# Token tile 1 on the ScalarE queue, and a later fill of block 1's second and third w1 chunks

## The chip, the cores and the metric

The kernel runs on one core of one Trainium2 chip. The metric is device time in microseconds (us) of one execution. The profile shows a *span*, from the first to the last instruction of the program, which is shorter than the time by some 2 us. "Same" means within 2%.

Engines: PE is TensorE (PEld its weight loads), DVE is VectorE, ACT is ScalarE, POOL is GpSimd, SP is SyncE. A "q" after an engine's name (ACTq) means its instruction stream, where DMA transfers are issued.

## The reference, cut to what matters

```python
xn = layernorm(x)                        # x: (1, 2048, 512) bf16
q  = (xn @ wq) in 32 heads of 128
k, v = the last 512 cached keys and values, 8 heads, each used by 4 query heads
s  = softmax(q k^T / sqrt(128)) v, heads joined, @ wo
g  = silu( silu(xn @ w1) @ w2 )          # w1: 512 x 1792, w2: 1792 x 512
out = x + s * g
```

## The kernel before

The 2048 tokens are handled as 4 blocks of 512, a block as 4 tiles of 128. Block 0 opens with its own layernorm and the first MLP layer for its tokens (`h_pair`). After that each step of the loop is one attention head of one block, and single MLP matmuls ("fill") are slipped between the attention's matmuls so that PE does not run out of work. Two places are touched.

**Place A, the start.** Tile 0 goes out in halves on two queues, tile 1 on a third, tiles 2 and 3 on ScalarE's; the w1 pieces follow on SyncE's.

```python
    with tc.manual_schedule(engines={ENG.PE, ENG.Activation, ENG.DVE, ENG.SP, ENG.Pool}):
        ...
        nc.sync.dma_start(x_blk[0][0:HP4, 0, :], x0v[0:HP4, 0, :])
        nc.scalar.dma_start(x_blk[0][HP4:P, 0, :], x0v[HP4:P, 0, :])
        nc.gpsimd.dma_start(x_blk[0][:, 1, :], x0v[:, 1, :])              # tile 1
        make_identity(nc, ident)
        nc.gpsimd.memset(neg_half, -0.5)
        NE = NEARLY * P                                                   # 512
        nc.sync.dma_start(w1_sb[0][:, :, 0 : NE // 2], w1v[:, :, 0 : NE // 2])      # piece a
        nc.sync.dma_start(w1_sb[0][:, :, NE // 2 : NE], w1v[:, :, NE // 2 : NE])    # piece b
        nc.scalar.dma_start(x_blk[0][:, 2:4, :], x0v[:, 2:4, :])          # tiles 2 and 3
        nc.sync.dma_start(w1_sb[0][:, :, NE:], w1v[:, :, NE : FH * P])              # piece c
        nc.sync.dma_start(w1_sb[1][:, :, 0:NE], w1v[:, :, FH * P : FH * P + NE])    # second half, piece 1
        ...
        stats(0, 0)                    # VectorE: statistics of tile 0, then of tile 1, in order
        stats(0, 1)
        for j in range(2):
            rstd_first(j)              # ScalarE
            center(0, j)               # VectorE
        warm_up(10)                    # PE: dummy matmuls
        ...                            # PE: transposes of tiles 0 and 1
        for i in range(2 * FH):
            h_pair(i, i // FH)         # PE: 8 matmuls on tiles 0 and 1 (i < 7), then on 2 and 3
            if i == 3:
                t2 = turn(2)           # PE: transposes of tiles 2 and 3
                t3 = turn(3)
                ...
```

**Place B, the fill list.** `mlp_units` gives for a block a list `hs` of 14 x 4 matmuls (14 chunks of w1 columns, 4 matmuls each, one PSUM bank per chunk) and a list `os_` for the second layer. All use PSUM tag "f", which has two buffers. A chunk's bank is free again once ScalarE's tanh and one VectorE operation have read it. `pump(n)` issues the next n units.

```python
        fill = []
        for b in range(NBLK):
            hs, os_ = mlp_units(b, lambda i: "f")
            fill += hs * (b > 0) + os_
        ...
        def pump(n):
            nonlocal done
            for _ in range(n):
                if fill:
                    fill.pop(0)()
                    done += 1
```

The softmax here doesn't subtract the row's maximum and nothing guards it: scores larger than these inputs give would overflow.

Of the kernel before, what the change touches and what calls it, by code (L numbers as in the profile page):

```python
# [22 lines left out]
def kernel(  # L23
# [12 lines left out]
    nc = tc.nc  # L36
# [8 lines left out]
    ND = D // P  # L45
# [21 lines left out]
    warm = const.tile([P, BLK], BF16, name="warm")  # L67
    nc.vector.memset(warm, 0.0)
    ident = const.tile([P, P], BF16, name="ident")
    scratch = const.tile([P, 1], FP32, name="scratch")  # L70
    nc.vector.memset(scratch, 0.0)
    eps = const.tile([P, 1], FP32, name="eps")
    nc.vector.memset(eps, 1e-5)
    neg_half = const.tile([P, BLKT], FP32, name="neg_half")

    wq_sb = [res.tile([P, ND, REP * DH], BF16, name=f"wq{g}", tag=f"wq{g}") for g in range(HKV)]
    kT = [res.tile([P, W], BF16, name=f"kT{g}", tag=f"kT{g}") for g in range(HKV)]
# [13 lines left out]
    x_blk = {}  # L91
# [69 lines left out]
    def mlp_units(b, tag_of):  # L161

        cur = {}

        def h_unit(f, c):
            if (f, c) == (0, 0):
                new_hT(b)
            if c == 0:
                cur["ps"] = ps.tile([P, BLK], FP32, name="h_ps", tag=tag_of(f), bufs=PS_BUFS[tag_of(f)])
            h_mm(cur["ps"], b, f, c, 0, BLK)  # L170
            if c == ND - 1:
                h_evac(cur["ps"], b, f)

        def o_unit(j, f):
            if f == 0 and j == 0:
                g_sb[b] = res.tile([P, BLKT, D], BF16, name=f"gate{b}", tag=f"g{b}")
            if f == 0:
                cur["ps"] = ps.tile([P, D], FP32, name="oB_ps", tag=tag_of(j), bufs=PS_BUFS[tag_of(j)])
            nc.tensor.matmul(  # L179
                cur["ps"],  # L180
                hT[b][f // 2][:, f % 2, j * P : (j + 1) * P],
                w2_sb[f // FH][:, f % FH, :],
                start=(f == 0),
                stop=(f == NFC - 1),
            )
            if f == NFC - 1:
                th = work.tile([P, D], BF16, name="th", bufs=2)
                nc.scalar.activation(th, cur["ps"], ACT.Tanh, scale=0.25)
                nc.vector.scalar_tensor_tensor(  # L189
                    out=g_sb[b][:, j, :], in0=th, scalar=1.0, in1=cur["ps"], op0=ALU.add, op1=ALU.mult  # L190
                )

        hs = [lambda f=f, c=c: h_unit(f, c) for f in range(NFC) for c in range(ND)]
        os_ = [lambda j=j, f=f: o_unit(j, f) for j in range(BLKT) for f in range(NFC)]
        return hs, os_
# [417 lines left out]
    with tc.manual_schedule(engines={ENG.PE, ENG.Activation, ENG.DVE, ENG.SP, ENG.Pool}):  # L613
        new_x(0)
        x0v = x2[ds(0, BLK), :].rearrange("(j p) d -> p j d", p=P)
        nc.sync.dma_start(x_blk[0][0:HP4, 0, :], x0v[0:HP4, 0, :])  # L616
        nc.scalar.dma_start(x_blk[0][HP4:P, 0, :], x0v[HP4:P, 0, :])
        nc.gpsimd.dma_start(x_blk[0][:, 1, :], x0v[:, 1, :])
        make_identity(nc, ident)
        nc.gpsimd.memset(neg_half, -0.5)  # L620
        NE = NEARLY * P
        nc.sync.dma_start(w1_sb[0][:, :, 0 : NE // 2], w1v[:, :, 0 : NE // 2])  # L622
        nc.sync.dma_start(w1_sb[0][:, :, NE // 2 : NE], w1v[:, :, NE // 2 : NE])
# [95 lines left out]
        fill = []  # L719
        for b in range(NBLK):  # L720
            hs, os_ = mlp_units(b, lambda i: "f")
            fill += hs * (b > 0) + os_
        n_mlp = len(fill)
        done = 0

        def pump(n):
            nonlocal done
            for _ in range(n):
                if fill:
                    fill.pop(0)()  # L730
                    done += 1

        wo_plan = {
            HQ - 5: [(0, 4)],
# [35 lines left out]
        for s in range(NSTEP):  # L770
            b, h = divmod(s, HQ)
# [21 lines left out]
            if b == 0:  # L793
                units = S[0:1] + qu + S[1:2] + pu[:2] + S[2:3] + pu[2:] + S[3:4]
                for i, u in enumerate(units):
                    u()
                    pump((i + 1) * n // len(units) - i * n // len(units))
            else:
                for u in S[0:1] + qu + S[1:2] + pu + S[2:3]:
                    u()  # L800
                pump(2)
                S[3]()
                pump(2)
# [46 lines left out]
```

## Time and profile before

| | before |
|---|---|
| time, median of 3 runs | 550.3 us (549.86 to 550.56) |
| span of the profiled execution | 548.5 us |
| PE busy | 542.2 us, 99% of the span |
| granted clock of PE | 1.00 in the early stretches shown below |

The page of the kernel before, its first line, the first group of part 1 and part 4 (the chain of work that ended last, by engine):

```profile
span 548.5 us, 8534 instructions
PE 542.2 (99%) x2676; PEld 261.2 (48%) x2676; DVE 458.3 (84%) x1258; ACT 392.3 (72%) x1125; POOL 21.1 (4%) x42
...
PE 96%; DMA 1%; DVE 1%; SPq 0%; issue 0%; ACT 0%
```

PE is the limit. The view of the waits of PE from 0 to 46 us (us in total, times, longest):

```profile
PE warm_ps L642 <- DVE eps L73: 1.2, 1, 1.2
PE t_ps L649 <- DVE x_114 L122: 0.8, 1, 0.8
PE h_ps L691 <- DMA w_0_106<-in_B_w_dram: 0.2, 1, 0.2
PE h_ps L146 <- DVE gate_413 L189: 0.2, 1, 0.2
```

The second line is place A, the fourth is place B. The timeline of the start (columns: start, busy us, engine, line, operation, output<-input, and in brackets the idle time before with what ended it) shows why PE waits at A:

```profile
1.25 0.71 POOL L618 DMA_DIRECT2D x_114<-in_A_x_dram  x1 [0.81 <-POOLq L834]
...
4.85 0.69 DVE L107 BATCH_NORM_STATS2 st<-x_114 128x6 f32<-128x512 bf16 x1 [0.60 <-DMA x_114<-in_A_x_dram]
...
6.11 0.40 PE L649 MATMUL t_ps<-ident,x_114 128*128 128x128 bf16 x4 [0.83 <-DVE x_114 L122]
...
7.34 1.91 PE L691 MATMUL h_ps<-xnT_102,w_0_106 128*128 128x256 bf16 x16
...
9.44 1.49 PE L691 MATMUL h_ps<-xnT_102,w_0_106 128*128 128x256 bf16 x12 [0.20 <-DMA w_0_106<-in_B_w_dram]
...
11.39 0.61 PE L658 MATMUL t_ps<-ident,x_114 128*128 128x128 bf16 x8
```

Tile 1 is issued at 1.25 us and VectorE waits for it until 4.85 us; PE's first transposes come at 6.11 us after 0.83 us of idleness. Later, at 9.44 us, PE waits for a weight transfer all the same. The transposes of tiles 2 and 3 at 11.39 us will serve below as the mark of where the start ends.

DMA issues between 0 and 6 us (kind, count, KB, us from issue to landing), and the line of GB/s of that window in 40 slices of 0.15 us:

```profile
x_114<-in_A_x_dram POOLq DMA_DIRECT2D x1, 128.0 KB, 3.6
x_114<-in_A_x_dram ACTq DMA_DIRECT2D x1, 256.0 KB, 3.7
w_0_106<-in_B_w_dram SPq DMA_DIRECT2D x1, 384.0 KB, 6.6
...
GB/s 0 0 0 0 0 0 0 0 0 0 0 0 0 41 191 185 212 198 130 178 184 314 246 307 321 403 301 273 328 317 290 345 352 335 324 328 294 266 220 183
```

Place B, the timeline of VectorE and PE around 42 us:

```profile
41.58 0.68 DVE L189 SCALAR_TENSOR_TENSOR gate_413<-th,oB_ps 128x512 bf16<-128x512 bf16 x1
...
41.75 0.38 PE L146 MATMUL h_ps<-xnT_103,w_0_106 128*128 128x512 bf16 x1
42.30 0.38 PE L146 MATMUL h_ps<-xnT_103,w_0_106 128*128 128x512 bf16 x1 [0.18 <-DVE gate_413 L189]
```

Pipelined matmuls of this shape start 0.216 us apart in this stretch. Here the starts are 0.55 us apart, so the wait for the bank that `gate_413` empties costs 0.34 us, more than the recorded 0.18 us of idleness.

### The profile page before, as it was taken

What the parts mean: (1) busy time and instruction counts of PE and PEld (TensorE: products, weight loads), DVE (VectorE), ACT (ScalarE), POOL (GpSimd) and SP (SyncE); (2) the same over time, 40 slices, a digit from 0 to 9 for tenths busy, and PEclk for the clock granted to TensorE, in tenths of its full rate; (3) what the DMA queues carried; (4) which work ended last, traced back from release to release, by engine and by line L of the source; (5) the groups of instructions that cost most, each with busy time, mean ns of one, the idle gap of its engine ahead of it and who ended that gap; (6) DMA issues with size and microseconds to landing.
All of it is one profiled execution on the core that took longest, in us unless ns stands there. A gap on an engine that the chain in (4) does not pass through costs nothing.

```text
span 548.5 us, 8534 instructions
## 1 busy us (share of the span) xinstructions
PE 542.2 (99%) x2676; PEld 261.2 (48%) x2676; DVE 458.3 (84%) x1258; ACT 392.3 (72%) x1125; POOL 21.1 (4%) x42
## 2 busy tenths in 40 slices
PE   8999999999999999999999999999999999999997
PEld 5644444444444444444444444444444444444586
DVE  6878888887886688898889888988889889988897
ACT  5558767766785677777777777777788888888600
POOL 1000010000000000010001000100010000100010
PEclk9999999999999999999999999999999999999999
DMA  8969669797849799989887988898888878888921
GB/s 270 261 115 190 151 136 163 147 164 149 167 89 185 178 213 220 199 161 190 162 149 149 183 167 141 162 184 160 148 162 179 153 153 157 186 154 154 173 78 39
DMA packets 298813, 89.69 MB, mean 164 GB/s; under 512 B 282352, under 2 KB 297840, under 8 KB 298768
## 3 DMA queue, kind: packets, MB, share of 16 engines
q1 hardware_dynamic: 297056, 85.02, 79.4%
q0 software_dynamic: 1360, 3.80, 2.7%
q8 instruction: 21, 0.34, 0.2%
q10 hardware_dynamic: 352, 0.33, 0.2%
q14 instruction: 24, 0.20, 0.1%
HBM read 17.30 MB, written 2.10 MB: 35 GB/s over the span
## 4 chain that ended last, share of the span: by engine, by line
PE 96%; DMA 1%; DVE 1%; SPq 0%; issue 0%; ACT 0%
PE o_ps L275 20%; PE q_ps L210 20%; PE sc_ps L232 20%; PE s_ps L333 15%; PE oB_ps L179 8%; PE h_ps L146 7%; PE m_ps L476 4%; PE h_ps L691 2%; DMA w_0_106<-in_B_w_dram 1%; DVE gate_413 L189 0%; DVE p_all L247 0%; DVE st L107 0%; SPq L622 0%; DVE qT L222 0%; SPq L616 0%
## 5 line engine op out<-in xcount | busy, mean ns | idle before, releaser
L235 ACT ACTIVATE p_all<-sc_ps 128x512 bf16<-128x512 f32 x512 | 305.3, 597 | 104.3 <-PE sc_ps L232 100.3
L247 DVE TENSOR_SCALAR p_all<-p_all,rden 128x512 bf16<-128x512 bf16 x512 | 157.9, 351 | 9.1
L281 DVE CAST oT<-o_ps 128x512 bf16<-128x512 f32 x128 | 88.2, 689 | 35.8 <-PE o_ps L275 35.2
L235 ACT ACTIVATION_READ_ACCUMULATOR p_all<-sc_ps 128x1 f32 x512 | 100.4, 196 | 0.0
L232 PEld LDWEIGHTS <-qT 128*128 128x128 bf16 x512 | 50.1, 98 | 60.7 <-issue 0.5
L222 DVE CAST qT<-q_ps 128x512 bf16<-128x512 f32 x111 | 76.3, 687 | 3.3 <-PE q_ps L210 3.3
L333 PEld LDWEIGHTS <-oT 128*128 128x128 bf16 x384 | 37.6, 98 | 45.3
L245 DVE RECIPROCAL rden<-den 128x2 f32<-128x2 f32 x256 | 40.6, 158 | 11.2 <-ACT p_all L235 11.0
L156 ACT ACTIVATE th<-h_ps 128x512 bf16<-128x512 f32 x42 | 25.0, 595 | 4.0 <-PE h_ps L146 3.9
L333 PE MATMUL s_ps<-wo_big_2083,oT 128*128 128x512 bf16 x84 | 26.0, 379 | 0.0
L333 PE MATMUL s_ps<-wo_big_2084,oT 128*128 128x512 bf16 x84 | 26.0, 379 | 0.0
L333 PE MATMUL s_ps<-wo_big_2344,oT 128*128 128x512 bf16 x84 | 26.0, 379 | 0.0
L333 PE MATMUL s_ps<-wo_big_2345,oT 128*128 128x512 bf16 x84 | 26.0, 379 | 0.0
L232 PE MATMUL sc_ps<-kT_86,qT 128*128 128x512 bf16 x64 | 24.3, 379 | 0.0
L232 PE MATMUL sc_ps<-kT_87,qT 128*128 128x512 bf16 x64 | 24.3, 379 | 0.0
L232 PE MATMUL sc_ps<-kT_88,qT 128*128 128x512 bf16 x64 | 24.3, 379 | 0.0
L232 PE MATMUL sc_ps<-kT_89,qT 128*128 128x512 bf16 x64 | 24.3, 379 | 0.0
L232 PE MATMUL sc_ps<-kT_90,qT 128*128 128x512 bf16 x64 | 24.3, 379 | 0.0
L232 PE MATMUL sc_ps<-kT_91,qT 128*128 128x512 bf16 x64 | 24.3, 379 | 0.0
L232 PE MATMUL sc_ps<-kT_92,qT 128*128 128x512 bf16 x64 | 24.3, 379 | 0.0
L232 PE MATMUL sc_ps<-kT_93,qT 128*128 128x512 bf16 x64 | 23.9, 379 | 0.0
L350 POOL DMA_DIRECT2D out_dram<-x_e x12 | 6.6, 550 | 314.5 <-DVE rden L245 257.9
(317 smaller groups left out, 871.1 us busy)
## 6 DMA issues: line engine op xcount, KB each, us to landing
pT<-p_all SPq DMA_TRANSPOSE x128, 4.4
x_e<-in_A_x_dram POOLq DMA_DIRECT2D x12, 128.0 KB, 3.3
out_dram<-x_e POOLq DMA_DIRECT2D x12, 128.0 KB, 2.2
w_0_108<-in_B_w_dram SPq DMA_DIRECT2D x1, 896.0 KB, 9.5
w_1_109<-in_B_w_dram SPq DMA_DIRECT2D x1, 896.0 KB, 9.8
w_0_106<-in_B_w_dram SPq DMA_DIRECT2D x2, 256.0 KB, 4.8
w_1_107<-in_B_w_dram SPq DMA_DIRECT2D x1, 512.0 KB, 7.6
x_130<-in_A_x_dram SPq DMA_DIRECT2D x1, 512.0 KB, 9.6
```

The costliest lines, as they stand in the source:

```text
L146: nc.tensor.matmul(h_ps[:, lo : lo + n], w1_sb[f // FH][:, c, (f % FH) * P : (f % FH + 1) * P], xnT[b][:, c, lo : lo + n], start=(c == 0), ...
L156: nc.scalar.activation(th, h_ps, ACT.Tanh, scale=0.5)
L179: nc.tensor.matmul(cur["ps"], hT[b][f // 2][:, f % 2, j * P : (j + 1) * P], w2_sb[f // FH][:, f % FH, :], start=(f == 0), stop=(f == NFC - 1),
L210: nc.tensor.matmul(cur["ps"], wq_sb[h // REP][:, c, (h % REP) * DH : (h % REP + 1) * DH], xnT[b][:, c, :], start=(c == 0), stop=(c == ND - 1),
L222: nc.vector.tensor_copy(qT[s], cur["ps"])
L232: nc.tensor.matmul(sc, qT[s][:, j * P : (j + 1) * P], kT[h // REP], start=True, stop=True)
L235: nc.scalar.activation(p_all[s][:, :, j, :], sc.rearrange("p (kc q) -> p kc q", q=P), ACT.Exp, scale=INV_SQRT_DH, accum_out=den[s][:, j : ...
L245: nc.vector.reciprocal(rden, den[s][:, j0 : j1 + 1])
L247: nc.vector.tensor_scalar_mul(p_all[s][:, :, j, :], p_all[s][:, :, j, :], rden[:, j - j0 : j - j0 + 1])
L275: nc.tensor.matmul(cur["ps"], v_sb[h // REP][:, kc, :], pT[s][:, kc, :], start=(kc == 0), stop=(kc == NKC - 1))
L281: nc.vector.tensor_copy(oT[s // 2][:, s % 2, :], cur["ps"])
L333: nc.tensor.matmul(acc[j], oT[(b * HQ + h) // 2][:, h % 2, j * P : (j + 1) * P], wo_of(h), start=(h == 0), stop=(h == HQ - 1),)
```

## The change

Three parts. Tile 1 goes to ScalarE's queue, to be there earlier. The two constants are made on GpSimd before the hand-ordered part, since nothing precedes them there any more. In block 1, two empty turns are put before the second chunk, so that its bank is free when PE comes to it; the third chunk then catches up, two matmuls a turn.

```diff
     ident = const.tile([P, P], BF16, name="ident")
+    make_identity(nc, ident)
     ...
     neg_half = const.tile([P, BLKT], FP32, name="neg_half")
+    nc.gpsimd.memset(neg_half, -0.5)
...
-        nc.gpsimd.dma_start(x_blk[0][:, 1, :], x0v[:, 1, :])
-        make_identity(nc, ident)
-        nc.gpsimd.memset(neg_half, -0.5)
+        nc.scalar.dma_start(x_blk[0][:, 1, :], x0v[:, 1, :])
...
             hs, os_ = mlp_units(b, lambda i: "f")
-            fill += hs * (b > 0) + os_
+            if b == 1:
+
+                late = [lambda u=hs[i : i + 2]: [x() for x in u] for i in (2 * ND, 2 * ND + 2)]
+                fill += hs[:ND] + [None, None] + hs[ND : 2 * ND] + late + hs[3 * ND :] + os_
+            else:
+                fill += hs * (b > 0) + os_
...
                 if fill:
-                    fill.pop(0)()
+                    u = fill.pop(0)
                     done += 1
+                    if u is not None:
+                        u()
```

## The prediction

> **What bounds the kernel.** TensorE. The page gives PE 542.2 us of a 548.5 us span (99%), and the chain of waits that ended last is 96% PE. PE lacks work only before its first matmul (1.18 us), at a few points up to 11 us, once at 42 us, and in the closing evacuation. The change removes no matmul, so it can only win idle PE time, at two places.
>
> **Place A, the start (timeline 0 to 12 us).** Token tile 1 of x goes out on the GpSimd queue at 1.25 us and lands 3.6 us later; VectorE, in order, waits 0.60 us for it, until 4.85 us, and so centres tile 0 only at 5.67 us, although its rstd is ready at 4.57 us. PE idles 0.83 us before the first transposes (6.11 us); the first MLP matmul is at 7.34 us. On the ScalarE queue I expect the issue at about 1.3 us and landing near 4.3 us (the 64 KB piece there took 2.2 us, the 256 KB one 3.7 us). Tiles 2 and 3 go out 0.6 us later (one issue) and land near 5.5 us; their statistics start after 6.5 us, so that is harmless. First transposes and first MLP matmul come about 0.5 us earlier.
> But most of that is off the critical path: the chain runs through the third piece of w1's first half, issued at 2.78 us, landing at 9.44 us, where PE waits 0.20 us; next, the first piece of the second half holds a weight load at 10.94 us. From 3 us on the DMA engines are full (share about 1.0, 260 to 365 GB/s) and the bytes ahead of these pieces stay the same. The Trainium skill, "DMA: Bandwidth & Descriptors", section "Issuing engines are not separate DMA queues", says that all queues run on the same 16 engines, so another queue adds no bandwidth. PE will mostly wait longer near 9.4 us. Only what the weights land earlier counts: 0.2 us (0 to 0.5).
>
> **Place B, block 1's first MLP fill (40 to 46 us).** The only PE wait found after 11 us is at 42.30 us: the second w1 chunk needs the PSUM bank that VectorE empties (gate evacuation, 41.58 to 42.27 us). Recorded idle is 0.18 us; by start-to-start spacing (0.55 us against the usual 0.216) it is 0.34 us. In the changed order only one score matmul more stands between the first and second chunk, so the second is reached near 42.18 us: about 0.1 us of wait is left. The third, two at a time, catches up; from the fourth the order is as before. The fourth needs the second's bank: 0.57 us until tanh, 0.6 tanh, 0.69 VectorE puts that near 45.7 us, against a demand near 45.5 us, so up to 0.2 us can come back there. Net 0.15 us (0 to 0.3).
>
> **Moved for nothing:** identity and the -0.5 constant on GpSimd; done by 2.6 us, first needed at 6.1 and 9.3 us.
>
> **Sum.** 0.35 us off 550.3; the runs before spread by twice that. Predicted 549.9 us, range 549.2 to 550.6; chances: faster by over 2% 0.005, within 2% 0.99, slower 0.005.
>
> **What would show it.** Right: tile 1 lands before 4.5 us; first MLP matmul near 6.8 us; a longer PE wait for w1 near 9 us; the 42.3 us gap at about 0.1 us, perhaps a small new one near 45.6 us; all after 50 us shifted by a constant 0.2 to 0.6 us. Wrong: w1 landing half a microsecond earlier (the software queue was costing bandwidth: 549.4 or less) or later (tile 1 competes earlier), or a new gap near 45.6 us eating B.

## More of the kernel before

The output matrix `wo` is loaded in portions of rows by SyncE, each portion one transfer; two experiments join or split portions of this plan only to change the *number* of transfers.

```python
        wo_plan = {
            HQ - 5: [(0, 4)],
            HQ - 4: [(4, 3)],
            HQ - 3: [(7, 4)],
            HQ - 2: [(11, 3)],
            ...
```

## The result, and the profile after

| | before, same rounds | after |
|---|---|---|
| median of 6 runs | 549.99 us (549.33 to 550.56) | 549.95 us (549.88 to 550.32) |
| ratio | | 1.0001, 95% interval 0.9988 to 1.0014: same |
| profiled span | 548.5 us | 547.7 us |

A ratio is the mean time of one kernel's fast runs over that of the other's in the same rounds, so it is not quite the ratio of the medians in the table. The interval is about 0.7 us to either side.

The predicted number, 549.9 us, was met. Yet there is something to explain: the span fell by 0.8 us and the time by nothing. The page of the kernel after:

```profile
span 547.7 us, 8533 instructions
PE 542.2 (99%) x2676; PEld 261.1 (48%) x2676; DVE 458.4 (84%) x1258; ACT 392.1 (72%) x1125; POOL 20.5 (4%) x41
...
PE 98%; DMA 1%; SPq 0%; DVE 0%; issue 0%
```

The waits of PE from 0 to 46 us are down to two:

```profile
PE warm_ps L642 <- DVE eps L74: 1.2, 1, 1.2
PE h_ps L691 <- DMA w_0_111<-in_B_w_dram: 0.2, 1, 0.2
```

The timeline of the start, the same instructions as before:

```profile
1.32 0.60 ACTq L620 DMA_DIRECT2D x_119<-in_A_x_dram  x1
...
4.12 0.66 DVE L109 BATCH_NORM_STATS2 st<-x_119 128x6 f32<-128x512 bf16 x1
...
5.36 0.40 PE L649 MATMUL t_ps<-ident,x_119 128*128 128x128 bf16 x4
...
6.58 1.99 PE L691 MATMUL h_ps<-xnT_107,w_0_111 128*128 128x256 bf16 x16
...
8.72 1.48 PE L691 MATMUL h_ps<-xnT_107,w_0_111 128*128 128x256 bf16 x12 [0.16 <-DMA w_0_111<-in_B_w_dram]
...
10.68 0.61 PE L658 MATMUL t_ps<-ident,x_119 128*128 128x128 bf16 x8
```

Every mark is 0.7 us earlier, the first transposes (5.36 instead of 6.11 us) as well as the end of the start (10.68 instead of 11.39 us). Taken alone this reads as a full win of 0.7 us. The DMA issues of 0 to 6 us, and the GB/s of that window, say something else:

```profile
x_119<-in_A_x_dram ACTq DMA_DIRECT2D x1, 128.0 KB, 2.5
x_119<-in_A_x_dram ACTq DMA_DIRECT2D x1, 256.0 KB, 4.6
w_0_111<-in_B_w_dram SPq DMA_DIRECT2D x1, 384.0 KB, 5.9
...
GB/s 0 0 0 0 0 0 0 0 0 0 0 0 0 20 171 246 191 226 191 300 318 171 79 65 75 106 160 123 133 229 314 277 341 348 372 376 355 352 362 345
```

Tile 1 is at hand 2.5 us after its issue instead of 3.6. Tiles 2 and 3 take 4.6 us instead of 3.7. Between 3.3 and 4.2 us, where the kernel before moved some 300 GB/s, the DMA engines now move 65 to 160.

Place B after the change, PE's timeline:

```profile
41.03 0.38 PE L148 MATMUL h_ps<-xnT_108,w_0_111 128*128 128x512 bf16 x1
41.25 0.38 PE L234 MATMUL sc_ps<-kT_91,qT 128*128 128x512 bf16 x1
41.59 0.38 PE L148 MATMUL h_ps<-xnT_108,w_0_111 128*128 128x512 bf16 x1
...
44.61 0.38 PE L277 MATMUL o_ps<-pT,v_99 128*128 128x512 bf16 x1
44.89 0.38 PE L148 MATMUL h_ps<-xnT_108,w_0_111 128*128 128x512 bf16 x1
```

By spacing, the wait ahead of the second chunk is now 0.34 - 0.216 = 0.12 us (it was 0.34), and a new one of 0.28 - 0.216 = 0.06 us stands ahead of the fourth chunk.

So there were three questions. Is the 0.7 us of the start real? What is B worth over the whole kernel? And where does the time go between the span and the time?

### The profile page after: what moved, and what is told of

Read it like the earlier page. It is cut to its first block, busy times and chain, and to the rows that moved or that the text cites. A ratio compares the mean times of both kernels' runs of the same rounds, so it can differ in the third digit from the quotient of the medians.

```text
span 547.7 us, 8533 instructions
## 1 busy us (share of the span) xinstructions
PE 542.2 (99%) x2676; PEld 261.1 (48%) x2676; DVE 458.4 (84%) x1258; ACT 392.1 (72%) x1125; POOL 20.5 (4%) x41
## 3 DMA queue, kind: packets, MB, share of 16 engines
q0 software_dynamic: 1312, 3.67, 2.6%
## 4 chain that ended last, share of the span: by engine, by line
PE 98%; DMA 1%; SPq 0%; DVE 0%; issue 0%
PE o_ps L277 20%; PE q_ps L212 20%; PE sc_ps L234 20%; PE s_ps L335 15%; PE oB_ps L181 9%; PE h_ps L148 7%; PE m_ps L478 4%; PE h_ps L691 2%; DMA w_0_111<-in_B_w_dram 1%; SPq L622 0%; SPq L618 0%; SPq L623 0%; PE t_ps L658 0%; DVE m_4_6595 L502 0%; DVE x_t L604 0%
## 5 line engine op out<-in xcount | busy, mean ns | idle before, releaser
L277 PE MATMUL o_ps<-pT,v_100 128*128 128x512 bf16 x64 | 18.4, 379 | 0.0
```

The costliest lines, as they stand in the source:

```text
L277: nc.tensor.matmul(cur["ps"], v_sb[h // REP][:, kc, :], pT[s][:, kc, :], start=(kc == 0), stop=(kc == NKC - 1))
```

## The experiments

All kernels gave the right result. The letters in the expectations are these theories. **Q**: tile 1's earlier landing gains the whole 0.7 us seen in the first two profiles. **J**: the first profile of the kernel before fell on an execution with a late start, and the real gain is smaller. For what lies outside the span: **G**, it hangs on GpSimd's instruction stream; **S**, on ScalarE's; **C**, on the constants made early. **R**: the end of the program waits through a fixed list, and one more transfer moves the last output in it. **W**: the w1 pieces land later because the early transfers use two queues instead of three.

### Both kernels again, and each half of the change alone (5 rounds each)

e1 is the kernel before and e2 the kernel after, both unchanged. e3 is the change without its fill part; e4 is the kernel before with only the fill part.

```diff
# e3, against the kernel after
-            if b == 1:
-                ...
-                fill += hs[:ND] + [None, None] + hs[ND : 2 * ND] + late + hs[3 * ND :] + os_
-            else:
-                fill += hs * (b > 0) + os_
+            fill += hs * (b > 0) + os_
# e4, against the kernel before: the same lines the other way round, queue and constants as before
```

> The kernel before, unchanged, as a second look at its start. Theory J (jitter): the landing of the third w1 piece (9.44 us in the first profile) moves by half a microsecond or more from execution to execution, whatever the kernel, and the span with it; then this profile shows another landing time, and span minus landing time is the same as in the first profile (548.5 - 9.44 = 539.1 us) within 0.1 us. Rival Q (the queue really gains 0.7 us, the equal medians are chance): landing again at 9.4 us, span 548.5 us, and the kernel after is 0.8 us faster in this job.

> The changed kernel again. Theory Q: third w1 piece lands near 8.7 us again, span 547.7 us, 0.8 us under the kernel before. Theory J: the landing differs from 8.72 us; span minus landing stays at 547.7 - 8.72 = 539.0 us; mean time within 0.3 us of the kernel before.

> Only the queue of token tile 1 (and the earlier GpSimd constants); the fill order as before. The wait at 42 us (0.34 us by spacing) is back whole. Theory Q: span about 547.8 to 547.9 us, 0.6 to 0.7 us under before. Theory J: mean time equal to before within 0.3 us; first transposes near 5.4 us, but the third w1 piece wherever the DMA puts it. Prediction on record: 0.2 us faster.

> Only the fill order; token tile 1 stays on the GpSimd queue. Both theories: the wait at 42 us shrinks from 0.34 to 0.12 us by spacing and 0.06 us comes back at the fourth chunk, so 0.16 us less from 40 to 46 us. Theory Q: time 0.16 us under before. Theory J: the same on average, but hidden in a spread of 0.5 us or more from the start.

| run | median us (range) | ratio to the kernel before, 95% interval |
|---|---|---|
| e1, before again | 549.69 (549.19 to 550.31) | 0.9985, 0.9968 to 1.0002 |
| e2, after again | 550.01 (549.72 to 550.21) | 0.9990, 0.9972 to 1.0008 |
| e3, queue only | 550.41 (549.67 to 551.1) | 0.9997, 0.9980 to 1.0015 |
| e4, fill only | 549.8 (549.34 to 550.0) | 0.9985, 0.9969 to 1.0002 |
| the kernel before beside them (11 runs) | 550.33 (549.33 to 552.75) | |

The kernel before against itself gave 0.9985, so that is the size of the noise: none of these times tells the parts apart. The traces do. This is the page's first line and PE's timeline of the start in the repeated run of the kernel before (e1):

```profile
span 547.7 us, 8534 instructions
...
5.64 0.40 PE L649 MATMUL t_ps<-ident,x 128*128 128x128 bf16 x4 [0.20 <-DVE x L122]
6.87 3.88 PE L691 MATMUL h_ps<-xnT,w 128*128 128x256 bf16 x32
10.58 0.61 PE L658 MATMUL t_ps<-ident,x 128*128 128x128 bf16 x8
```

The same kernel that had started its first transposes at 6.11 us and ended its start at 11.39 us now does so at 5.64 and 10.58 us, and its span is 547.7 us, that of the changed kernel. In this execution no wait of PE for w1 is recorded: its 32 matmuls run on from 6.87 us, in 3.88 us (3.65 us in e6, e8, e9 and e11). The six spans of e1 lie between 547.4 and 548.5 us; those of e2 between 547.4 and 547.9. In e2 the third w1 piece landed at 8.83 us, close to the 8.68 us of the first look, as Q had expected too; it is e1 that decides. J stands and Q falls: the first profile of the kernel before was a late one.

From block 1's first fill matmul to VectorE's last operation, on the other hand, the trace gives the same number every time for each fill order:

```
fill order   kernel    first fill matmul   last VectorE op   difference, us
old          before         40.67              545.24            504.57
old          e1             39.86              544.42            504.56
old          e3             40.05              544.62            504.57
new          after          39.95              544.36            504.41
new          e2             40.12              544.52            504.40
new          e4             40.09              544.49            504.40
```

B is worth 0.16 us, which is what the two gaps at 42 and 45 us add up to (0.34 - 0.12 - 0.06). From PE's transposes of tiles 2 and 3 to that first fill matmul it is 29.28 us in before (11.39 to 40.67) and in e1 (10.58 to 39.86), and 29.27 us in after. So the trace is rigid from 11 us to VectorE's last operation, and the start can be read from one mark.

In e4, which has the old start, time minus span was small again; in e3, which has the new start, it was as in e2. That led to the next set.

### What lies outside the span (e5 in 5 rounds, e6 to e8 one look each)

Time minus span is 2.29 us (2.23 to 2.40, 24 runs) in the kernels in which tile 1 left GpSimd's queue with nothing in its place (after, e2, e3, e6, e10), and 1.78 us (1.72 to 1.89, 59 runs) where GpSimd issues an early load. These four runs were to say which engine's stream it hangs on. All edits are small:

```diff
# e5: the kernel after, with two dummy memsets, so that GpSimd's stream is as long as before
+    pad = const.tile([P, 1], FP32, name="pad")
+    for _ in range(2):
+        nc.gpsimd.memset(pad, 0.0)
# e6: the kernel before, tile 1 on SyncE's queue
-        nc.gpsimd.dma_start(x_blk[0][:, 1, :], x0v[:, 1, :])
+        nc.sync.dma_start(x_blk[0][:, 1, :], x0v[:, 1, :])
# e7: the kernel before, with make_identity and the memset of neg_half moved up as in the change
# e8: the kernel before, with one more instruction on ScalarE
         nc.scalar.activation(scratch, scratch, ACT.Tanh)
+        nc.scalar.activation(scratch, scratch, ACT.Tanh)
```

> The changed kernel with two dummy GpSimd memsets at its start, so that GpSimd has 70 instructions again as before the change (68 in the changed kernel). In all runs so far the time lies 1.79 us over the span of the program's own instructions with token tile 1 on the GpSimd queue, and 2.30 us with it on the ScalarE queue: half a microsecond is given back outside the span. Theory G (it hangs on the length of GpSimd's instruction stream): 1.8 us again, and the time 0.5 us under the changed kernel, near 549.5 us. Theory S (on ScalarE's stream, one instruction longer) and theory C (on the early constants): 2.3 us, time near 550.0 us.

> The kernel before with token tile 1 on the SyncE queue: GpSimd two instructions shorter, ScalarE as before, constants where they were. Time minus span: theory G 2.3 us; theories S and C 1.8 us.

> The kernel before with only the identity and the -0.5 constant made early; token tile 1 still on the GpSimd queue, behind them. Time minus span: theory C 2.3 us; theories G and S 1.8 us. At the start token tile 1 lands later than in the kernel before (about 0.3 us), and by theory J the third w1 piece and the first transposes of tiles 2 and 3 still fall into the range seen so far (10.6 to 11.4 us for the latter).

> The kernel before with one more ScalarE instruction (the table-warming tanh on 128x1 twice, 0.2 us). Time minus span: theory S 2.3 us; theories G and C 1.8 us.

| run | instructions on GpSimd | time us | span us | time minus span us |
|---|---|---|---|---|
| before | 70 | 550.36 (profiled run) | 548.5 | 1.78 (mean of 59 runs of its kind) |
| after | 68 | 549.95 (profiled run) | 547.7 | 2.29 (mean of 24 runs of its kind) |
| e5 | 70 | 549.95 median, 549.71 to 550.21 | 548.3 | 1.77 (6 runs, 1.72 to 1.81) |
| e6 | 68 | 550.34, one run | 548.0 | 2.34 |
| e7 | 70 | 549.97, one run | 548.2 | 1.77 |
| e8 | 70 | 549.44, one run | 547.7 | 1.74 |

(The count is of all records of GpSimd's stream, issues and register work included, and so is above the 42 and 41 of the page.) G stands: two idle memsets bring the difference back to 1.77 us, and neither ScalarE's stream (e8) nor early constants (e7) change it; e6, with ScalarE's stream untouched, has the large difference. S and C fall. One expectation of e7 was missed: tile 1 landed at 4.68 us there, not later than in before (4.82 us); its mark, 11.07 us, lay in the range expected.

But I had expected e5 to take 549.5 us, and it took 549.95, as the kernel after does. Half a microsecond came back outside the span and the span grew. The semaphore records of SyncE at the end of the program say how. Times are ns before the end of the span; each line of waits is worked through by SyncE in the order given:

```
before  last output issued -2817
        waits: -2421 S105, -2367 S106 S104, -2306 S107 S103, -2242 S109 S102, -2180 S111 S101,
               -2121 S112 S100, -2059 S114 S99, -2000 S115 S108, -1938 S117 S113, -1260 S118 S116
        the last output's landing counts S118 up until -1277; SyncE drains -1192, -1132
after   last output issued -2867
        waits: -2470 S117, -2417 S118 S116, -1310 S100 S115, -1246 S102 S114, -1184, -1125,
               -1063, -1004, -943, -883 S110 S109
        the last output's landing counts S100 up until -1327; SyncE drains -816, -756
```

SyncE waits for all semaphores in a fixed order, some 62 ns each. The hardware queues' transfers take eight of these semaphores in turn. Before, the last output of the kernel had the eighth, S118, and all other waits were done while it was still on its way: 0.145 us after it had landed (-1277 to -1132) SyncE was through. Tile 1 on ScalarE's queue is one more transfer of this kind, so every later one moves by one, the last output comes to the first of the eight, S100, and seven more waits have to be worked through *after* it has landed: 0.571 us (-1327 to -756). The view of SyncE's waits from 543 us on shows the same, before and after:

```profile
SPq L845 <- DMA out_dram<-x_t: 0.6, 1, 0.6
...
SPq L852 <- DMA out_dram<-x_t: 1.1, 1, 1.1
```

Before, SyncE comes to the wait for the last output when the others are done, and waits 0.6 us; after, it comes to it earlier, waits 1.1 us and still has seven waits to go. This is theory R. It costs 0.571 - 0.145 = 0.43 us. e5 has the same 0.571 us (-1713 to -1142); it hid in the span there.

And G is mostly a move. With 70 instructions GpSimd waits 0.41 us inside the span ahead of the last barrier, with 68 it waits 0.04 us there and a gap after the span is 0.5 us longer. From SyncE's second drain to the end of the time it is 1.13 + 1.79 = 2.92 us before and 0.76 + 2.29 = 3.05 us after: 0.13 us to the bad. In the single profiled runs this stretch takes 2.89 to 2.99 us with 70 instructions (9 runs, e5 among them) and 3.03 to 3.12 us with 68 (5 runs). What is waited for after the span, the trace doesn't show.

### Changing the number of transfers (e10 in 5 rounds, e11 one look), and two more

R can be tried without touching the start at all. e10 joins two loads of `wo` in the kernel after, so that the last output is back on the eighth semaphore. e11 adds four transfers to the kernel before, so that it comes to the fourth.

```diff
# e10, against the kernel after
-            HQ - 3: [(7, 4)],
-            HQ - 2: [(11, 3)],
+            HQ - 3: [(7, 7)],
# e11, against the kernel before
-            HQ - 5: [(0, 4)],
-            HQ - 4: [(4, 3)],
+            HQ - 5: [(0, 1), (1, 1), (2, 1), (3, 1)],
+            HQ - 4: [(4, 1), (5, 2)],
```

> The changed kernel with two loads of wo in the middle (4 and 3 heads) made one of 7 heads: one hardware-queue transfer fewer, as many as before the change; its start is untouched and GpSimd keeps 68 instructions. Theory R: last landing to drain 0.14 us, time minus span still 2.3 us, time 0.43 us under the changed kernel, near 549.6 us. Theory Q2 (the end is longer because of what the start does): 0.57 us, time 550.0 us.

> The kernel before with two loads of wo in the middle cut into six: four hardware-queue transfers more. Theory R: the last output takes the fourth of the eight semaphores, four more waits of 62 ns follow its landing, so landing to drain is 0.14 + 0.25 = 0.39 us; time minus span 1.8 us. Q2: 0.14 us.

| run | last output landed, to SyncE's second drain | expected by R |
|---|---|---|
| e10 | 0.144 us (-906 to -762) | 0.14 |
| e11 | 0.386 us (-1533 to -1147), fourth of the eight, S112 | 0.39 |
| e8, for comparison (same number of transfers as before) | 0.144 us | 0.14 |
| e6, for comparison (same number as after) | 0.570 us (-1332 to -762) | 0.57 |

SyncE's wait in e10 is the short one again:

```profile
SPq L851 <- DMA out_dram<-x_t: 0.6, 1, 0.6
```

R is shown: one transfer fewer, at about 175 us, takes 0.43 us out of the end of the kernel. The time agrees: e10's median is 549.54 us (549.4 to 549.8, 5 runs), its mean 549.61 us, where the 12 runs of the kernel after have a mean of 550.03 us (standard deviation 0.18), 0.42 us more. Those were taken in other jobs (e2's on another chip), and against the kernel before of its own rounds e10 is 0.9992 (0.9979 to 1.0005), where e2 was 0.9990: set against their own rounds, the times do not tell the two apart. So the proof is the trace. e11 took 550.37 us in its one run, with a span of 548.5 us.

e9 tests the transfers at the start: tile 1 on ScalarE's queue as in the change, and tiles 2 and 3 on GpSimd's, so that three queues are used again. e12 is e4 once more.

```diff
# e9, against the kernel after
         nc.scalar.dma_start(x_blk[0][:, 1, :], x0v[:, 1, :])
+        nc.gpsimd.dma_start(x_blk[0][:, 2:4, :], x0v[:, 2:4, :])
...
-        nc.scalar.dma_start(x_blk[0][:, 2:4, :], x0v[:, 2:4, :])
```

> The changed kernel, but tiles 2 and 3 of block 0 go on the GpSimd queue while tile 1 stays on ScalarE's: as many hardware-queue transfers as before the change. Theory R (the end list): SyncE waits at the end for every semaphore in a fixed order; hardware-queue transfers take eight semaphores in turn, so one transfer more moves the last output from the last place of the list to the third, and seven more waits of 62 ns (0.43 us) run after it has landed. Here it is back at the last place: last landing to the SyncE drain 0.14 us as in the kernel before (0.57 in the changed one), GpSimd 70 instructions, time minus span 1.8 us. Start, theory W (the weights pay for tile 1: with two queues instead of three 400 to 450 KB are in at 4.5 us instead of 510 to 620): here three queues again, tile 1 lands before 4 us, the first w1 pieces by 6.1 and 7.2 us. Time near 549.5 us, 0.5 us under the changed kernel. Rival: no recovery at the end (end 0.57 us), time 550.0 us.

> The fill order alone again, to compare with the two repairs in one job. 0.16 us under the kernel before where their starts are alike; mean 549.7 to 550.1 us, with a wider spread (0.4 us or more) than kernels that load tile 1 on the ScalarE queue (0.18 us in twelve runs of the changed one).

e12 gave 550.03 us (549.52 to 550.19, 5 runs), ratio 0.9997 (0.9985 to 1.0009), and once more 545.02 - 40.62 = 504.40 us from the first fill matmul to the last VectorE operation. So the 0.16 us of B is exact in every trace and invisible in the time.

e9 ran four times in 548.94 to 549.38 us, three of these the fastest runs of the whole study, and twice in 552.45 and 552.67 us, with a granted clock of 0.997 in both. Its ratio is 1.0004 (0.9981 to 1.0028). Its start ended at 10.33 us and its last output was on S118 again. Whether its typical gain would hold could not be settled: runs of over 551.2 us also came up in the kernel before (one at 552.75 us). There were 7 in 59 runs of kernels with an early load on GpSimd's queue, and none in 30 runs without one, though the slowest of these, one of e3 at 551.1 us, is just under that limit. That may be chance, and no run here was made to decide it.

### The start, over all traces

PE's start on the transposes of tiles 2 and 3, the mark of the start's end, and KB moved by the DMA engines up to 4.5 us:

```
tile 1 on GpSimd's queue     mark us   KB        tile 1 on ScalarE's queue   mark us   KB
before                        11.39    596       after                        10.68    402
e1                            10.58    602       e2                           10.84    454
e4                            10.81    612       e3                           10.77    454
e8                            10.55    514       e5                           10.92    438
e11                           11.13    559       e10                          10.92    415
e12                           11.34    564
mean                          10.97              mean                         10.83
range                          0.84              range                         0.24
(e7, constants early: 11.07, 618)                (e6, SyncE's queue: 10.82, 602; e9: 10.33, 532)
```

The new order gains 0.14 us in the mean, with a standard error of 0.16 us by the scatter of these marks: an estimate that is not clear of zero. What shows better is steadiness: the marks lie within 0.24 us instead of 0.84. In the times even that is not shown: e3, with the new start, ran from 549.67 to 551.1 us.

Why only so little, when tile 1 lands a whole microsecond earlier? The w1 pieces land later. Pieces a and b of its first half came at 5.65 to 6.37 and 6.61 to 7.21 us in the traces of the left column, and at 6.18 to 6.84 and 7.47 to 7.72 us in those of the right one. In the typical trace of either kernel it is then piece c that PE runs into: in 11 of the 14 traces the mark comes 2.00 to 2.03 us after c has landed (in e8, e9 and e11 later, 2.08 to 2.43 us). From its landing to the end of the span it is 539.12 us in before (548.51 - 9.39), 539.13 in e1, 539.00 in after (547.68 - 8.68), 539.02 in e2 and 538.96 in e4: with B's 0.16 us taken off, one constant. e8, where piece c landed at 8.12 us, is above it, 539.56 us, as PE itself was the limit there.

In after the later landing goes with the hole in the GB/s line between 3.3 and 4.2 us. In the trace, tiles 2 and 3 (issued at 1.95 us) get their first data only at about 4.2 us, and piece a, in packets of 512 bytes, has the engines nearly to itself: the first 288 of its packets start over 1.42 us, where in before they did so over 0.74. Theory W, that this comes of having two queues for three, stays open. e6 also used two and moved 602 KB by 4.5 us, as much as before, so two queues alone do not empty the engines; but there piece a was issued one transfer later (2.24 instead of 1.37 us), and pieces a, b and c landed as late as in the new order (6.82, 7.66 and 8.81 us). e9, with three queues, met W's expectation for pieces a and b (6.12 and 6.93 us), and not that for tile 1 (4.32 us instead of before 4). What the five traces of the new order share is an order: piece a, issued at 1.37 us, starts at 3.04 to 3.09 us, and tiles 2 and 3, issued at 1.95 us, only at 3.67 to 4.30 us; in before, tiles 2 and 3 were issued first and started at 2.59 us, piece a at 3.94 us. Whether the order or the number of queues counts, no run settled. The Trainium skill, "Perfetto Trace Analysis", section "DMA Instruction — HWDGE (DVE, Sync)", describes a block that makes descriptors, is shared by two sequencers (the page's diagram names VectorE's and SyncE's, its note SyncE's and ScalarE's, which issue here) and is locked by one of them while in use. The late first data of tiles 2 and 3 agree with that, but do not show it.

## Why the prediction was right or wrong

**The number: right by luck.** Predicted 549.9 us, measured 549.95 us. The prediction took 0.35 us off a base of 550.3 us, the median of three runs. With three runs more the base is 549.99 us, and of the predicted gain only 0.04 us shows in the medians (549.99 to 549.95 us in the same rounds), with an interval of 0.7 us to either side.

| term | predicted | measured | read from |
|---|---|---|---|
| A, the start | -0.2 us (0 to -0.5) | -0.14 us, an estimate, not clear of zero | marks of 6 and 5 traces |
| B, the fill | -0.15 us (0 to -0.3) | -0.16 us | the 504.57 and 504.40 us |
| place in the end's list of waits | not seen | +0.43 us | e10, e11, e5, e6 |
| GpSimd's shorter stream at the end | not seen | +0.13 us | 2.92 and 3.05 us |
| sum | -0.35 us | +0.26 us | |

The sum of +0.26 us and the measured difference of about nothing agree within the interval of 0.7 us. Over all jobs the kernel before has a median of 549.94 us (39 runs) and the kernel after 549.97 us (12 runs).

**PE is the limit, and only idle PE time can be won: right up to the last matmul.** PE was busy for 542.2 us in both kernels. But e10 wins 0.43 us behind the last matmul, where no PE work is left.

**Place A, the mechanism: right in outline.** "Most of that is off the critical path" held: tile 1's landing came about 1 us earlier, and the end of the start 0.14 us. The details: tile 1 lands at 3.79 us (predicted near 4.3), the first MLP matmul comes at 6.58 us (predicted near 6.8). The predicted "longer PE wait for w1 near 9 us" is not there in the first pair of traces: 0.20 before, 0.16 after. Part of it is inside the first matmul group, which takes 1.99 instead of 1.91 us, but the main reason is that the first profile of before was a late execution. Over all traces the prediction is right: such a wait is recorded in four of the five traces of the new order (0.16 us in after and e3, 0.4 in e5, twice 0.15 or more in e10; none in e2), and in those with tile 1 on GpSimd's queue only in before.

**"From 3 us on the DMA engines are full and the bytes ahead of these pieces stay the same": wrong for the changed kernel.** The windows view of before and of after at 3.5 to 4.5 us shows it (columns: window, busy us and count of PE, PEld, DVE, ACT, POOL, then granted clock, DMA share, GB/s). Before:

```profile
3.50:4.00 0.50, 0.50 (x2) 0.15 (x1) 0.50 (x1) 0.00 (x0) 0.00 (x0) 1.00 0.88 324
4.00:4.50 0.50, 0.50 (x2) 0.15 (x1) 0.21 (x2) 0.22 (x1) 0.00 (x0) 1.00 1.01 315
```

After:

```profile
3.50:4.00 0.50, 0.50 (x2) 0.15 (x1) 0.49 (x1) 0.21 (x1) 0.00 (x0) 1.00 0.41 98
4.00:4.50 0.50, 0.50 (x2) 0.15 (x1) 0.48 (x2) 0.26 (x1) 0.00 (x0) 1.00 0.58 162
```

A share of 0.41 is not full. The prediction took the load of the DMA engines before the change for a property of the hardware's limit, and leaned on the Trainium skill, "DMA: Bandwidth & Descriptors", section "Issuing engines are not separate DMA queues", for the queue making no difference to the bandwidth. Over a longer stretch the traces nearly agree with that page: by 6.5 us 1158 KB had been moved before and 1073 KB after. By 4.5 us it was 596 and 402 KB.

**"Tiles 2 and 3 land near 5.5 us; harmless": wrong by 1 us, and harmless.** They landed at 1.95 + 4.6 = 6.55 us; VectorE's statistics on them began at 6.62 us, where PE was already busy with its first MLP matmuls.

**Place B: right in size and in place.** The wait at 42.3 us fell to 0.12 us (predicted about 0.1), and the new one before the fourth chunk is 0.06 us (predicted up to 0.2). It came at 44.9 us; the prediction put it near 45.5. Net 0.16 us (predicted 0.15).

**"Moved for nothing: identity and the -0.5 constant": right** (e7: 549.97 us in one run, time minus span 1.77 us as before).

**The step that failed** is the one that isn't in the prediction: it costed only what precedes the last matmul, and took what follows it as unchanged. The change added one transfer to the hardware queues and took two instructions off GpSimd, and these cost 0.43 and 0.13 us at the end, by this sum more than A and B had won. The 0.43 us are shown by experiment (e10, e11). Why a shorter GpSimd stream costs 0.13 us stays open, and whether the whole change gains or loses, the times cannot tell.

## What to carry to other kernels

When a change is worth tenths of a microsecond, add up everything that it alters *after* the last output as well as before: the number of transfers alone decided whether seven waits of 62 ns stood behind the last landing, and a load joined in the middle of the kernel (e10) took them away. Read several profiles of the unchanged kernel before believing a difference between two single ones: here its span ran from 547.4 to 548.5 us in six runs. And look at the first transfer on the critical path, not at the one that was moved: here tile 1 landed about 1 us earlier and the w1 pieces that PE needed landed later.

## What the Trainium skill lacked or had wrong

- No page that I read has the list of waits at the end of the program, as the traces show it: SyncE goes through the semaphores in a fixed order, about 62 ns apart here, and the place of the last output among eight semaphores in turn is worth up to 0.43 us (0.145 us after the landing where it is last, 0.386 us where it is fourth, 0.571 us where it is first). It would belong in "Runtime: NRT & Kernel Launch", section "The launch sequence".
- The same page and section (under "The ~15µs preamble/postamble breakdown") give the stages after the kernel, barriers and resets, with one amount each. Here the time outside the span was 1.78 us with 70 instructions on GpSimd and 2.29 us with 68, most of it shifted across the span's end (net 0.13 us). The cause is open.
- "DMA: Bandwidth & Descriptors", section "Issuing engines are not separate DMA queues", says that several issuing engines save only sequencer time. On the whole that nearly holds (1158 and 1073 KB by 6.5 us), but for the first microseconds of a kernel the queue and order of three transfers made 596 or 402 KB by 4.5 us. It would help to say so.
- The same page, section "Latency and other measured facts", gives about 0.6 us to the first byte for hardware queues and about 1 us for the software queue. From the start of the issue to the first packet the trace of the kernel before has 1.34 us on ScalarE (0.73 to 2.08 us), 1.6 us on SyncE and 1.75 us on GpSimd (1.25 to 3.00 us). The order agrees; the amounts, which here include the issue itself, are larger. Counted from the end of the issue they are 0.79, 1.02 and 1.04 us.
